# Recurrent attention and a GELU feed-forward on one core: another tiling, another order of transfers, and a list schedule of small groups

## The chip, the cores and the metric

The kernel runs on one core of a Trainium2 chip. The metric is the device time of one execution in microseconds (us). Three runs of the kernel before gave a median of 257.52 us (257.4 to 257.78).

## The reference

For 4 batches of 8 heads, 768 steps of 48 channels, a state of 48 x 48 decays by channel and takes in one outer product at each step; then follow two matrix products with a GELU between them. Cut to what is computed:

```python
f = 1.0 / (1.0 + np.exp(-f_logit))
state = np.zeros((B, H, D, D), dtype=np.float32)
for t in range(S):
    state = f[:, :, t, :, None] * state + np.einsum('bhd,bhe->bhde', k[:, :, t], v[:, :, t])
    y[:, :, t] = np.einsum('bhd,bhde->bhe', q[:, :, t], state)
x = np.ascontiguousarray(y.transpose(0, 2, 1, 3)).reshape(B * S, H * D)
h = x @ w_in                                      # 3072 x 384 by 384 x 2048
g = 0.5 * h * (1.0 + erf(h / np.sqrt(2.0)))
out = g @ w_out                                   # 2048 x 384
```

## The kernel before

The 3072 tokens are 24 chunks of 128 positions, six to a batch. Each chunk needs four loads of 192 KB (f_logit, k, q, v; rows of 48 numbers), an attention part and a feed-forward part.

The decays of a chunk: exponential (L291) and logarithm (L294) on ACT give log f; one matmul with a triangle of -1 (L304) sums it over the positions; two exponentials (L307, L311) give the factors `gt` and `rg`; four matmuls of one column per chunk (L334) and a small exponential (L338) give the decay `gl` over the whole chunk.

The attention, in line order: DVE scales k and q (L314, L318); PE transposes both for four pairs of heads (L361); DVE copies the transposed k into a zero-padded tile in two halves of 48 partitions (L367), ACT copies q (L370); eight score matmuls over all 128 rows (L380), where the zero rows of `kb` blank out the other head of the pair; DVE applies the causal mask (L384). The state is formed by L397, decayed on DVE and GpSimd (L408 to L414) and cast (L421). The output is written with channels on partitions, so that each of eight matmuls (L435) and four state reads (L439) streams 128 positions; four DVE casts (L448, L451), three of them on 32 partitions, make `xT`, the input of the feed-forward.

The feed-forward works on groups of 1, 1, 2, 4, 4, 4, 4 and 4 chunks. "F1" is L473 (weights `win` stationary, `xT` streaming, 384 matmuls in all), GELU is L477 on ACT, "F2" is L488 (`gT` stationary, `wout` streaming 384 columns, 384 matmuls), then a copy on ACT (L492) and a store issued from SP (L494). F1 and F2 of all groups share four PSUM banks with the cumulative sums; the transposes have one bank (`tp`), the output one (`yp`).

The order is made by a planner, `Plan.run`: every operation has an engine, a duration, a priority and its dependences, and the one that can start earliest is placed next; each engine then runs its list in that fixed order. In the second half of `tile_hgrn2_outer__then__act_gelu_exact_kernel` locks are added: the exponentials of group g wait for the last GELU of group g-2 (`gate`), and the F1 and GELU of a group of four wait for the cumulative sums and exponentials of the next group (`lockpe`, `lock`). Loads of chunks are issued from SP, `win` (24 pieces of 16 rows, `load_win`) and `wout` (4 pieces) from GpSimd.

Of the kernel before, what the change touches and what calls it, by code (L numbers as in the profile page):

```python
# [14 lines left out]
class Ring:  # L15


    def __init__(self, bufs, make=None, fixed=None):
        self.bufs, self.make, self.fixed, self.order = bufs, make, fixed, []

    def new(self, **kw):
        return Buf(self, kw)


class Buf:
    def __init__(self, ring, kw):
        self.ring, self.kw, self.users, self.slot, self.handle = ring, kw, [], None, None

    def ready(self):

        r = self.ring
        if self.slot is not None or len(r.order) < r.bufs:
            return 0.0
        old = r.order[len(r.order) - r.bufs]
        t = 0.0
        for u in old.users:
            if u.end is None:
                return None
            t = max(t, u.vis)
        return t  # L40

    def take(self):
        if self.slot is None:
            self.slot = len(self.ring.order) % self.ring.bufs
            self.ring.order.append(self)

    def t(self):
        if self.handle is None:
            r = self.ring
            self.handle = r.fixed[self.slot] if r.fixed else r.make(**self.kw)  # L50
        return self.handle


LAT = {"PE": 0.28, "ACT": 0.12, "DVE": 0.12, "POOL": 0.15, "DMA": 2.0}
SWITCH = 1.28


class Op:
    __slots__ = ("eng", "dur", "fn", "bufs", "prio", "deps", "table", "start", "end", "vis", "seq", "name")


class Plan:

# [4 lines left out]
    def add(self, eng, dur, fn, rd=(), wr=(), bufs=(), prio=0.0, deps=(), table=None, name=""):  # L68
        o = Op()
        o.eng, o.dur, o.fn, o.bufs, o.prio, o.table, o.name = eng, dur, fn, tuple(bufs), prio, table, name  # L70
        o.start = o.end = o.vis = None
# [17 lines left out]
    def run(self):  # L89
        free = {e: 0.0 for e in LAT}  # L90
        act = None
        left = list(self.ops)
        placed = []
        while left:
            best = None
            for o in left:
                t, ok = free[o.eng], True
                for d in o.deps:
                    if d.end is None:
                        ok = False  # L100
# [14 lines left out]
                if o.table and act and o.table != act:  # L115
                    x += 2 * SWITCH
# [13 lines left out]
            for b in o.bufs:  # L130
                b.take()
            left.remove(o)
            placed.append(o)
        placed.sort(key=lambda o: (o.start, o.seq))
        self.placed = placed
        return placed


@with_exitstack
def kernel(  # L140
# [18 lines left out]
    P2 = H // 2  # L159
    KO = 3  # L160
    VB = 144
    PSUM = bass.MemoryType.PSUM
    SIZES = [1, 1, 2, 4, 4, 4, 4, 4]
    NG = len(SIZES)
    first = [sum(SIZES[:i]) for i in range(NG)]

    ctx.enter_context(tc.manual_schedule())
    one = ctx.enter_context(tc.tile_pool(name="one", bufs=1))
    ld = ctx.enter_context(tc.tile_pool(name="ld", bufs=8))
    lg = ctx.enter_context(tc.tile_pool(name="lg", bufs=3))  # L170
    el = ctx.enter_context(tc.tile_pool(name="el", bufs=3))
    at = ctx.enter_context(tc.tile_pool(name="at", bufs=3))
    fx = ctx.enter_context(tc.tile_pool(name="fx", bufs=3))
# [385 lines left out]
```

## Time and profile before

| | before |
|---|---|
| median of three runs | 257.52 us |
| the profiled execution, its span | 260.6 us |
| PE busy | 199.9 us, 77% |
| ACT busy | 152.8 us, 59% |
| DVE busy | 124.3 us, 48% |
| GpSimd busy | 58.9 us, 23% |
| mean granted TensorE clock | 0.895 |
| moved by DMA | 27.00 MB |

The profiled execution has no other time of its own than its span, from the first to the last instruction. It is 3.1 us above the median of the runs, which were not profiled. Busy time of PE counts a matmul from its start to its modelled end, so a busy PE can still be slow; the granted clock, 1.0 for 2.4 GHz and 0.5 for 1.2 GHz, stands beside it. All times in rows are microseconds from the start of the span unless marked ns.

### The profile page before, as it was taken

How to read it: one execution, taken by the hardware profiler on the slowest of the kernel's cores; microseconds unless marked ns; L12 is line 12 of the kernel's file. 1: busy time of each engine (PE TensorE's matmuls, PEld its weight loads, DVE VectorE, ACT ScalarE, POOL GpSimd, SP SyncE). 2: the span in 40 equal slices, each digit the busy share in tenths (PEclk: the TensorE clock that was granted, in tenths of full speed). 3: DMA queues.
4: the chain of work that ended last, by engine and by line, in shares of the span. 5: the costliest groups of instructions: out<-in, count | busy, mean ns of one | idle time of the engine just before them, and what ended most of it. 6: DMA issues, size and time to landing. Idle time of an engine off the chain costs nothing.

```text
span 260.6 us, 4299 instructions
## 1 busy us (share of the span) xinstructions
PE 199.9 (77%) x1611; PEld 130.5 (50%) x1624; DVE 124.3 (48%) x268; ACT 152.8 (59%) x243; POOL 58.9 (23%) x129
## 2 busy tenths in 40 slices
PE   0420739799157769898799999088996999999994
PEld 0310737577036555565475656045664665564462
DVE  5430057730049897993379720038973799200000
ACT  5620575545783852879735851977789456626911
POOL 8863052311020142330133300011130312000000
PEclk9999956999957576999689999759999899999999
DMA  8999919489999999998849302000000010011011
GB/s 140 187 190 184 146 14 168 64 182 202 215 188 186 187 166 193 188 164 132 170 107 209 64 0 93 30 1 0 3 0 33 30 64 0 0 63 60 0 60 60
DMA packets 106195, 27.00 MB, mean 104 GB/s; under 512 B 100672, under 2 KB 105792, under 8 KB 106176
## 3 DMA queue, kind: packets, MB, share of 16 engines
q1 hardware_dynamic: 103296, 23.60, 52.8%
q0 software_dynamic: 2880, 3.15, 8.0%
q8 instruction: 12, 0.20, 0.3%
q14 instruction: 7, 0.06, 0.1%
HBM read 25.17 MB, written 4.72 MB: 115 GB/s over the span
## 4 chain that ended last, share of the span: by engine, by line
PE 55%; ACT 16%; DVE 10%; DMA 8%; issue 5%; POOL 3%; ACTq 0%; POOLq 0%; DVEq 0%
PE hps L473 21%; PE hps L488 19%; DMA win<-in_moe_w_in_dram 7%; PE tp L361 4%; PE yp L435 3%; PE aps L380 3%; ACT lf L294 3%; ACT L294 2%; DVE xT L451 2%; ACT fl L291 2%; DVE kb L367 2%; ACT L291 2%; DMA wout<-in_moe_w_out_dram 2%; ACT qT L370 2%; PE hps L304 2%
## 5 line engine op out<-in xcount | busy, mean ns | idle before, releaser
L473 PE MATMUL hps<-xT,win 128*128 128x512 bf16 (+2 forms) x371 | 73.1, 341 | 13.5 <-DMA win<-in_moe_w_in_dram 11.5
L488 PE MATMUL hps<-wout,gT 128*128 128x384 bf16 x384 | 70.2, 337 | 1.7 <-DMA wout<-in_moe_w_out_dram 1.7
L477 ACT ACTIVATE gT<-hps 128x512 bf16<-128x512 f32 x96 | 55.1, 600 | 26.7 <-PE hps L473 24.4
L473 PEld LDWEIGHTS <-win 128*128 128x128 bf16 x384 | 34.7, 104 | 36.1 <-issue 10.8
L488 PEld LDWEIGHTS <-gT 128*128 128x128 bf16 x384 | 38.0, 101 | 28.1 <-issue 6.3
L314 DVE TENSOR_TENSOR kp<-kt,rg 128x384 bf16<-128x384 f32 x24 | 13.8, 574 | 71.5 <-ACT rg L311 71.2
L492 ACT ACTIVATE osb<-hps 128x384 f32<-128x384 f32 x24 | 11.7, 489 | 42.2 <-PE hps L488 42.2
L384 DVE TENSOR_TENSOR am<-aps,mask 128x512 bf16<-128x512 f32 x48 | 31.3, 687 | 8.2 <-PE aps L380 7.7
L414 POOL TENSOR_TENSOR tn<-rr,gl 128x384 f32<-128x384 f32 x16 | 13.4, 835 | 85.3 <-DVE rr L412 85.3
L370 ACT ACTIVATE qT<-tp 128x512 bf16<-128x512 bf16 x24 | 14.3, 596 | 29.8 <-PE tp L361 19.5
L304 PE MATMUL hps<-lf,trin 128*128 128x384 bf16 x24 | 9.2, 429 | 24.4 <-ACT lf L294 21.6
L380 PE MATMUL aps<-qT,kb 128*128 128x128 bf16 x192 | 19.1, 239 | 9.8 <-DVE kb L367 4.9
L326 POOL CAST vp<-vt 128x384 bf16<-128x384 f32 x24 | 12.3, 514 | 55.6 <-issue 24.5
L367 DVE COPY kb<-tp 48x512 bf16<-48x512 bf16 x48 | 20.2, 421 | 8.0 <-ACT qT L370 5.5
L435 PE MATMUL yp<-am,vp 128*128 128x128 bf16 x192 | 22.4, 239 | 1.3 <-DVE am L384 1.3
L380 PEld LDWEIGHTS <-kb 128*128 128x128 bf16 x192 | 14.3, 108 | 17.2 <-DVE kb L367 13.5
L451 DVE CAST xT<-yp 32x128 bf16<-32x128 f32 x72 | 20.6, 286 | 1.2
L435 PEld LDWEIGHTS <-vp 128*128 128x128 bf16 x192 | 17.3, 107 | 7.1 <-issue 2.3
L421 POOL CAST sb<-tn 48x192 bf16<-48x192 f32 x40 | 15.0, 376 | 13.7 <-DVE tn L408 11.7
L439 PE MATMUL yp<-qT,sb 128*128 128x128 bf16 x80 | 16.9, 236 | 0.0
L448 DVE CAST xT<-yp 96x384 bf16<-96x384 f32 x24 | 13.3, 552 | 6.6 <-PE yp L439 4.7
L334 PEld LDWEIGHTS <-lf 128*128 128x128 bf16 x96 | 3.9, 103 | 22.5 <-issue 22.3
(40 smaller groups left out, 197.1 us busy)
## 6 DMA issues: line engine op xcount, KB each, us to landing
fl<-in_f_logit_dram SPq DMA_DIRECT2D x24, 192.0 KB, 4.5
kt<-in_k_dram SPq DMA_DIRECT2D x24, 192.0 KB, 4.5
qt<-in_q_dram SPq DMA_DIRECT2D x24, 192.0 KB, 4.5
vt<-in_v_dram SPq DMA_DIRECT2D x24, 192.0 KB, 4.5
out_dram<-osb SPq DMA_DIRECT2D x24, 192.0 KB, 1.9
win<-in_moe_w_in_dram POOLq DMA_DIRECT2D x24, 64.0 KB, 5.6
wout<-in_moe_w_out_dram POOLq DMA_DIRECT2D x4, 384.0 KB, 5.5
```

The source lines that it names most:

```text
L304: P.add("PE", 0.17, lambda gps=gps, j=j: nc.tensor.matmul(gps.t()[:, 0:H * D], trin, lf.t()[:, j, :, 0:D], start=True, stop=True), rd=[("l ...
L367: P.add("DVE", 0.42, lambda hh=hh: nc.vector.tensor_copy(kb.t()[64 * hh:64 * hh + D, :, hh, :], tp.t()[64 * hh:64 * hh + D, 0]), rd=[("tk" ...
L370: P.add("ACT", 0.6, lambda: nc.scalar.activation(qT.t(), tp.t()[:, 1], AF.Copy), rd=[("tq", n)], wr=[("qT", n)], bufs=[tp, qT], prio=pr + ...
L380: nc.tensor.matmul(ap_.t()[:, i * C:(i + 1) * C], kb.t()[:, p, hh, :], qT.t()[:, p, :], start=True, stop=True)
L384: P.add("DVE", 0.69, lambda ap_=ap_, am=am: nc.vector.tensor_tensor(am.t(), ap_.t().rearrange("p (h t) -> p h t", t=C), mask.unsqueeze(1). ...
L421: nc.gpsimd.tensor_copy(dst[:, :, :, 16 * hh:16 * hh + 16], tn.t()[64 * hh:64 * hh + D, :, D * hh:D * hh + D] .rearrange("q p (g y) -> q p ...
L435: nc.tensor.matmul(yp.t()[:, p, :], vwin(vp.t(), 2 * p + hh), ams[half].t()[:, 2 * (p % 2) + hh, :], start=(hh == 0), stop=(hh == 1 and c ...
L439: nc.tensor.matmul(yp.t()[:, p, :], osb.t()[:, p, :], qT.t()[:, p, :], start=False, stop=True)
L451: P.add("DVE", 0.29, lambda kk=kk: nc.vector.tensor_copy(xT.t()[96:128, kk, cols()], yp.t()[32 * kk:32 * kk + 32, 3, :]), rd=[("yp", n, 1) ...
L473: nc.tensor.matmul(hps.t()[:, i * tok:(i + 1) * tok], win[:, kk, fo * 128:(fo + 1) * 128], xT.t()[:, kk, 0:tok], start=(kk == 0), stop=(kk ...
L477: acts.append(P.add("ACT", 0.6, lambda u=u, hps=hps: nc.scalar.activation(view()[:, u * pk:(u + 1) * pk, :].rearrange("p a b -> p (a b)"), ...
L488: nc.tensor.matmul(op.t()[:, 0:d_model], view()[:, fo, s_ * C:(s_ + 1) * C], wout[:, fo, :], start=(fo == 0), stop=(fo == FO - 1))
```

## The change

The arithmetic stays; tiling, buffers, transfers and order are new.

- Outputs have positions on partitions: the masked scores are now the stationary operand, and v (48 columns per head) streams. One cast (`yb`) and three transposes on PE (`xmm`), with one copy of 384 elements, make `xT`.
- The transposed k and q leave PSUM in one DVE copy (`kq`). Score matmuls contract over 64 rows: head hh of a pair lies in partitions 64hh to 64hh+63 and writes a PSUM bank of its own.
- `win` comes in four column quarters, F1 waits for its quarter alone, and the hidden units are taken in steps of four columns (`col`); `wout` rows are permuted to match, so that a partition reads four whole rows.
- One list, `LOADS`, orders all input transfers: chunks 0 to 3, `win`, chunk 4, half of `wout`, chunk 5, the rest, then chunks 6 to 23. Where the queue changes between SP and GpSimd, the transfer waits for one two or three places earlier.
- Groups are of 1 and 2 chunks; exponentials and logarithms come per 1 or 2 chunks, in one ACT table that holds both, loaded by name.
- The locks and gates are gone; the planner has other latencies and durations, and picks any free buffer instead of a ring's next. PSUM is split into four banks for F1 and F2, two for scores, and two (`s_m`) for cumulative sums, transposes, state, output and output transpose.

Core of the diff:

```diff
+SIZES = [1, 1, 1, 1, 2, 2, 2, 2, 2, 2, 2, 2, 2, 2]
...
+ELS = [1, 1, 1, 1, 2, 2, 2, 2, 2, 2, 2, 2, 2, 2]
+LOADS = ['c0', 'c1', 'c2', 'c3', 'i0', 'i1', 'i2', 'i3', 'c4', 'o0', 'o1', 'c5', 'o2', 'o3']
+LOADS += [f"c{n}" for n in range(6, 24)]
...
-    SIZES = [1, 1, 2, 4, 4, 4, 4, 4]
...
+    s_fh, s_ap, s_m = Slots(4, banks[0:4]), Slots(2, banks[4:6]), Slots(2, banks[6:8])
...
+    P.add("ACT", 0.0, lambda: nc.scalar.preload_act_table_set("natural_log_exp_and_others"), table="exp", prio=-200)
...
-    r_tp = Ring(1, lambda: pp.tile([C, 2, P2, C], BF16, name="tp"))
-    r_yp = Ring(1, lambda: pp.tile([C, P2, C], F32, name="yp"))
...
-        for hh in range(2):
-            r = (2 * kk + hh) * D + 16 * g if g < 3 else (6 + hh) * D + 16 * kk
-            nc.gpsimd.dma_start(out=win[32 * g + 16 * hh:32 * g + 16 * hh + 16, kk, :],
-                                in_=moe_w_in[r:r + 16, :])
...
+            o.inst = issue()
+            if i and order[i - 1][0] != eng:
+                back = 3 if eng == "pool" else 2
+                for j in range(i - back, -1, -1):
+                    if order[j][0] != eng and order[j][1].inst is not None:
+                        tc.add_manual_dep(
+                            o.inst.ins, order[j][1].inst.ins.name,
+                            mybir.DependencyInfo(mybir.DependencyClass.Sync, mybir.DependencyReason.DATA),
+                            reason="one transfer after another")
+                        break
...
+    win_src = moe_w_in.rearrange("(kk p) f -> p kk f", p=C)
+    wo_src = moe_w_out.rearrange("(r p j) m -> r p j m", r=4, j=4)
...
+    for what in LOADS:
...
+        elif what[0] == "i":
+            load("pool", what, lambda m=m: nc.gpsimd.dma_start(
+                out=win[:, :, 512 * m:512 * m + 512], in_=win_src[:, :, 512 * m:512 * m + 512]),
...
+        else:
+            load("pool", what, lambda m=m: nc.gpsimd.dma_start(out=wout[:, 4 * m:4 * m + 4, :], in_=wo_src[m]),
...
+                def cum(gps=gps, lf=lf, j=j):
+                    nc.tensor.matmul(gps.t()[:, 0:HD], trin, lf.t()[:, j, :, 0:D], start=True, stop=True)
+                    for p in range(P2):
+                        nc.tensor.matmul(gps.t()[:, HD + p:HD + p + 1], lf.t()[:, j, 2 * p:2 * p + 2, :], negcol,
+                                         start=True, stop=True, skip_group_check=True)
...
+                P.add("ACT", 0.40, lambda gps=gps, rg=rg: nc.scalar.activation(
+                    rg.t(), gps.t()[:, 0:HD], AF.Exp, scale=-1.0),
+                    rd=[("g", n)], wr=[("rg", n)], bufs=[gps, rg], table="exp", prio=pr, name=f"RG{n}")
...
+        P.add("DVE", 0.61, lambda: nc.vector.tensor_copy(kq.t(), tpv()),
...
+        def amm():
+            for p in range(P2):
+                for hh in range(2):
+                    r = slice(64 * hh, 64 * hh + 64)
+                    nc.tensor.matmul(aps[hh].t()[:, p * C:(p + 1) * C], kq.t()[r, 0, p, :], kq.t()[r, 1, p, :],
+                                     start=True, stop=True)
...
-            P.add("DVE", 0.42, lambda hh=hh: nc.vector.tensor_copy(
-                kb.t()[64 * hh:64 * hh + D, :, hh, :], tp.t()[64 * hh:64 * hh + D, 0]),
...
-        P.add("ACT", 0.6, lambda: nc.scalar.activation(qT.t(), tp.t()[:, 1], AF.Copy),
...
+        def ymm():
+            on = True
+            if c:
+                for p in range(P2):
+                    nc.tensor.matmul(yp.t()[:, 96 * p:96 * p + 96], kq.t()[:, 1, p, :], osb.t()[:, p, :],
+                                     start=on, stop=False, skip_group_check=True)
+                    on = False
+            for hh in range(2):
+                for p in range(P2):
+                    h = 2 * p + hh
+                    nc.tensor.matmul(yp.t()[:, D * h:D * h + D], ams[hh].t()[:, p, :], vb.t()[:, D * h:D * h + D],
+                                     start=on, stop=(hh == 1 and p == P2 - 1), skip_group_check=True)
+                    on = False
...
+        P.add("DVE", 0.475, lambda: nc.vector.tensor_copy(yb.t(), yp.t()[:, 0:HD]),
...
+        def xmm():
+            for i in range(KO):
+                nc.tensor.transpose(xpv()[:, i, :], yb.t()[:, i * C:(i + 1) * C], ident)
...
+        P.add("DVE", 0.27, lambda: nc.vector.tensor_copy(xT.t()[:, :, j * C:(j + 1) * C], xpv()),
...
-        P.add("DVE", 0.55, lambda: nc.vector.tensor_copy(xT.t()[0:96, :, cols()], yp.t()[0:96, 0:3, :]),
-              rd=[("yp", n, 0), ("yp", n, 1)], wr=[("x", n, 3)], bufs=[yp, xT], prio=pr + 2, name=f"X{n}")
-        for kk in range(KO):
-            P.add("DVE", 0.29, lambda kk=kk: nc.vector.tensor_copy(
-                xT.t()[96:128, kk, cols()], yp.t()[32 * kk:32 * kk + 32, 3, :]),
...
+        def col(fo):
+            return win[:, :, 512 * (fo // 4):512 * (fo // 4) + 512].rearrange("p kk (c j) -> p kk j c", j=4)[:, :, fo % 4, :]
...
+                        nc.tensor.matmul(hps.t()[:, i * tok:(i + 1) * tok], col(fo)[:, kk, :],
+                                         xT.t()[:, kk, :], start=(kk == 0), stop=(kk == KO - 1))
...
-        if g >= 2 and SIZES[g - 2] == 4:
-            G[g]["gate"] = [G[g - 2]["lastgelu"]]
...
-            if SIZES[g - 1] == 4:
-                G[g - 1]["lock"] = G[g]["lastexp"]
-                G[g - 1]["lockpe"] = G[g]["cums"]
...
+    for ph in PHASES:
+        lo, hi = map(int, ph[1:].split(":"))
+        if ph[0] == "X":
+            gate = decays(lo, hi, [])
+            for n in range(lo, hi):
+                attn(n)
...
+            for g in range(lo, hi):
+                got += ffn_group(g, [])
...
+        if o.table and state.get("t") != o.table:
+            state["t"] = o.table
+            if o.dur:
+                nc.scalar.preload_act_table_set({"exp": "natural_log_exp_and_others", "gelu": "gelu_and_others"}[o.table])
```

How this moves instructions is seen at three places. On ACT, before, the start of the decays of a group of four: `fl` is f_logit, `lf` its logarithm, `hps` a PSUM bank, `qT` the copy of the transposed q.

```order
L492 ACTIVATE osb<-hps 128x384 x2
L291 ACT_TABLE_LOAD
L291 ACTIVATE fl<-fl 128x1536
L294 ACT_TABLE_LOAD
L294 ACTIVATE lf_92<-fl 128x32x48
L311 ACT_TABLE_LOAD
L311 ACTIVATE rg<-hps 128x384
L307 ACTIVATE gt<-hps 128x384
L338 ACTIVATE gl<-hps 128x16
L311 ACTIVATE rg<-hps 128x384
L307 ACTIVATE gt<-hps 128x384
```

After, one such phase between the GELUs of two groups (`gT` is the GELU's output, L504 the copy of an output).

```order
L490 ACTIVATE gT_180<-ps_184 128x512
L531 ACT_TABLE_LOAD
L341 ACTIVATE rg_131<-ps_190 128x384
L344 ACTIVATE gt_128<-ps_190 128x384
L347 ACTIVATE gl_133<-ps_190 128x4
L319 ACTIVATE fl_93<-fl_93 128x768
L504 ACTIVATE osb_165<-ps_185 128x384
L323 ACTIVATE lf_99<-fl_93 128x16x48
L341 ACTIVATE rg_129<-ps_189 128x384
L344 ACTIVATE gt_126<-ps_189 128x384
L347 ACTIVATE gl_134<-ps_189 128x4
L504 ACTIVATE osb_166<-ps_186 128x384
```

Three table loads at the start of a group's decays are one now, and the decays of later chunks and the copies of finished outputs stand among each other. The whole list of ACT has 14 table loads.

On GpSimd, before, the weights: `vp` is the cast v, `sb` the cast state.

```order
L254 DMA win<-in_moe_w_in_dram 16x2048 x6
L326 CAST vp_101<-vt 128x8x3x16
L254 DMA win<-in_moe_w_in_dram 16x2048 x6
L421 CAST sb_107<-tn 48x4x3x16 x2
L254 DMA win<-in_moe_w_in_dram 16x2048 x12
L326 CAST vp_102<-vt 128x8x3x16
L326 CAST vp_103<-vt 128x8x3x16
L414 TENSOR_TENSOR tn<-rr,gl 128x384
L421 CAST sb_108<-tn 48x4x3x16
L259 DMA wout<-in_moe_w_out_dram 128x4x384
```

After, the same place.

```order
L423 TENSOR_TENSOR tn_156<-rr_152,gl_134 128x384
L428 CAST sb_159<-tn_156 48x4x48 x2
L305 DMA win<-in_moe_w_in_dram 128x3x512
L358 CAST vb_119<-vt_88 128x384
L305 DMA win<-in_moe_w_in_dram 128x3x512
L423 TENSOR_TENSOR tn_154<-rr_153,gl_135 128x384
L428 CAST sb_157<-tn_154 48x4x48
L305 DMA win<-in_moe_w_in_dram 128x3x512
L428 CAST sb_157<-tn_154 48x4x48
L309 DMA wout<-in_moe_w_out_dram 128x1536
L358 CAST vb_120<-vt_89 128x384
L309 DMA wout<-in_moe_w_out_dram 128x1536 x2
```

The 24 pieces of `win`, 12 of them ahead of the first state cast, became four, behind the casts of the first three chunks; `wout` follows them at once.

On SP, before, the transfers of chunk 4 and the first store: `fl`, `kt`, `qt`, `vt` are loads, `out_dram` the stores of finished outputs.

```order
L277 DMA fl<-in_f_logit_dram 128x8x48
L281 DMA kt<-in_k_dram 128x8x48
L281 DMA qt<-in_q_dram 128x8x48
L281 DMA vt<-in_v_dram 128x8x48
L494 DMA out_dram<-osb 128x384
L277 DMA fl<-in_f_logit_dram 128x8x48
L281 DMA kt<-in_k_dram 128x8x48
```

After, the same, from chunk 4's v on.

```order
L302 DMA vt_89<-in_v_dram 128x8x48
L299 DMA fl_93<-in_f_logit_dram 128x8x48
L302 DMA kt_74<-in_k_dram 128x8x48
L302 DMA qt_82<-in_q_dram 128x8x48
L302 DMA vt_90<-in_v_dram 128x8x48
L299 DMA fl_94<-in_f_logit_dram 128x8x48
L302 DMA kt_75<-in_k_dram 128x8x48
L302 DMA qt_83<-in_q_dram 128x8x48
L506 DMA out_dram<-osb_163 128x384
L506 DMA out_dram<-osb_164 128x384
L302 DMA vt_91<-in_v_dram 128x8x48
L299 DMA fl_94<-in_f_logit_dram 128x8x48
```

The first store stood between chunks 4 and 5; the first two stand now ahead of the v load of chunk 6. On PE, F1 and F2 pieces stand between the attention steps up to chunk 23; behind its last transpose come 20 F2 matmuls and then four times 48 F1 and 32 F2.

## Rows read from the trace of the kernel before

**Rows 1.** The page's busy time, share and instructions of each engine.
```profile
PE 199.9 (77%) x1611; PEld 130.5 (50%) x1624; DVE 124.3 (48%) x268; ACT 152.8 (59%) x243; POOL 58.9 (23%) x129
```

**Rows 2.** Stages: length, busy PE, PEld, DVE, ACT, POOL, then clock, DMA share, GB/s.
```profile
0.00:53.00 53.00, 24.00 (x252) 19.91 (x253) 22.72 (x48) 25.52 (x38) 26.07 (x65) 0.90 0.93 135
53.00:66.50 13.50, 13.35 (x102) 9.60 (x101) 1.45 (x5) 6.42 (x12) 1.40 (x3) 1.00 1.10 204
66.50:98.00 31.50, 17.60 (x172) 13.52 (x172) 20.94 (x45) 22.34 (x33) 6.79 (x14) 0.68 1.27 189
98.00:152.90 54.90, 50.96 (x411) 31.73 (x417) 39.14 (x86) 35.57 (x59) 13.99 (x28) 0.90 0.84 144
...
163.40:180.00 16.60, 9.35 (x79) 5.79 (x80) 6.04 (x12) 13.11 (x19) 2.01 (x4) 0.69 0.03 12
180.00:226.00 46.00, 43.05 (x363) 26.74 (x366) 33.99 (x75) 33.61 (x56) 8.61 (x17) 0.96 0.05 18
226.00:260.60 34.60, 31.16 (x176) 17.03 (x174) 0.00 (x0) 14.11 (x26) 0.00 (x0) 1.00 0.13 46
```

**Rows 3.** The chain of waits, long pieces: start, length, what.
```profile
20.70 5.51 DMA win<-in_moe_w_in_dram
...
46.01 4.88 DMA wout<-in_moe_w_out_dram
...
66.94 1.28 ACT L291
...
69.74 1.28 ACT L294
```

**Rows 4.** The chain again, runs of PE matmuls at full clock.
```profile
52.30 0.67 PE hps L473 x12
52.97 0.65 PE hps L488 x4
...
55.91 5.24 PE hps L473 x48
...
89.85 0.40 PE hps L334 x16
...
187.68 0.45 PE tp L361 x8
...
226.06 10.40 PE hps L488 x64
```

**Rows 5.** ACT by line and shape: count, busy us, mean ns, idle before it.
```profile
L370 ACT ACTIVATE qT<-tp 128x512 bf16<-128x512 bf16 x24 | 14.3, 596 | 29.8 <-PE tp L361 19.5 <-DVE kb L367 9.4 <-PE yp L439 0.9
...
L294 ACT ACT_TABLE_LOAD x8 | 10.3, 1283 | 0.1
...
L338 ACT ACTIVATE gl<-hps 128x4 f32<-128x4 f32 x2 | 0.4, 182 | 0.0
```

**Rows 6.** DVE by line and shape.
```profile
L451 DVE CAST xT<-yp 32x128 bf16<-32x128 f32 x72 | 20.6, 286 | 1.2
L367 DVE COPY kb<-tp 48x512 bf16<-48x512 bf16 x48 | 20.2, 421 | 8.0 <-ACT qT L370 5.5 <-PE tp L361 1.5
...
L448 DVE CAST xT<-yp 96x384 bf16<-96x384 f32 x24 | 13.3, 552 | 6.6 <-PE yp L439 4.7 <-PE yp L435 1.3
```

**Rows 7.** Timeline of ACT at the start: the first load's end.
```profile
3.96 0.52 ACT L291 ACTIVATE fl<-fl 128x384 f32<-128x384 f32 x1 [1.94 <-DMA fl<-in_f_logit_dram]
```

**Rows 8.** Two more stages, columns as in rows 2.
```profile
7.00:26.00 19.00, 4.25 (x30) 2.92 (x30) 5.13 (x11) 5.65 (x9) 11.30 (x25) 1.00 1.28 186
...
98.00:147.00 49.00, 45.11 (x370) 28.43 (x375) 36.27 (x80) 31.14 (x52) 13.49 (x27) 0.89 0.94 162
```

**Rows 9.** The chain's last piece.
```profile
257.30 0.49 ACT osb L492
```

**Rows 10.** PE by line and shape: matmuls and weight loads.
```profile
L473 PEld LDWEIGHTS <-win 128*128 128x128 bf16 x384 | 34.7, 104 | 36.1 <-issue 10.8 <-DMA win<-in_moe_w_in_dram 6.4
...
L380 PE MATMUL aps<-qT,kb 128*128 128x128 bf16 x192 | 19.1, 239 | 9.8 <-DVE kb L367 4.9 <-ACT qT L370 4.8
```

More of the change, by code (lines that the diff above doesn't have):

```diff
@@ L12, with __init__, new, free @@
 ALU = mybir.AluOpType
[L15 to L22, printed above, removed]
[L25 to L55 removed]
+LAT = {"PE": 0.25, "ACT": 0.16, "DVE": 0.14, "POOL": 0.12, "DMA": 1.0}
+TABLE = 1.28
+class Slots:
+    def __init__(self, n, tiles=None):
+        self.n, self.tiles = n, tiles
+        self.who = [None] * n
+    def new(self):
+        return Buf(self)
+    def free(self):
+        out = []
+        for i, b in enumerate(self.who):
+            t = 0.0
+            if b is not None:
+                for u in b.users:
+                    if u.end is None:
+                        t = None
+                        break
+                    t = max(t, u.vis)
+            if t is not None:
+                out.append((t, i))
+        return sorted(out)
+class Buf:
+    __slots__ = ("slots", "users", "slot")
+    def __init__(self, slots):
+        self.slots, self.users, self.slot = slots, [], None
+    def t(self):
+        return self.slots.tiles[self.slot]
 class Op:
[L59 removed]
+    __slots__ = ("eng", "dur", "fn", "bufs", "prio", "deps", "table", "start", "end", "vis", "seq", "name",
+                 "left", "outs", "inst", "gate")
 class Plan:
@@ L263 @@
+    for i in range(3):
+        P.add("DVE", 0.2, lambda i=i: nc.vector.memset(
+            s_sb.tiles[i].rearrange("p a b -> p (a b)").bitcast(F32), 0.0), wr=[f"sbz{i}"], prio=-70)
+    z_lf = [f"lfz{i}" for i in range(3)]
+    z_kp, z_qp = [f"kpz{i}" for i in range(NQ)], [f"qpz{i}" for i in range(NQ)]
+    z_sb = [f"sbz{i}" for i in range(3)]
+    G = [dict(xT=s_xT[SIZES[g]].new(), gT=s_gT[SIZES[g]].new()) for g in range(NG)]
     grp = {}
@@ new lines, with load, fn @@
+    n = 0
+    els = []
+    for s in ELS:
+        els.append(dict(ns=list(range(n, n + s)), fl=s_fl.new(), lf=s_lf.new()))
+        for j in range(s):
+            X[n + j].update(el=els[-1], j=j)
+        n += s
+    for n in range(NCH):
+        for nm in ("kt", "qt", "vt"):
+            X[n][nm] = s_in[nm].new()
+    order = []
+    def load(eng, what, issue, wr, bufs, dur, name):
+        i = len(order)
+        o = P.add("DMA", dur, None, wr=wr, bufs=bufs, prio=i, name=name)
+        o.table = None
+        order.append((eng, o))
+        def fn():
+            o.inst = issue()
[7 more added lines that the diff above has]
+                            reason="one transfer after another")
+                        break
+        o.fn = fn
+        return o
```

434 lines of the change are left out of this document (181 added, 253 removed).

## The prediction

> **What bounds the kernel now.** I read the page's busy line first, then the table of stages, then the chain of waits for what starts and ends each stage, then the groups by line for prices. PE is the busiest engine, yet busy for only 199.9 of 260.6 us [rows 1]. Cut into stages [rows 2], its 60.7 us of idle time lie mostly in three places: 29.0 us before 53 us, 13.9 us from 66.5 to 98 us, and 7.3 us from 163.4 to 180 us. In the last two the granted clock was 0.68 and 0.69 besides, so what PE did there cost half as much again. At 226 to 257 us nothing interrupts PE at all.
>
> The chain says what ends each gap [rows 3]. Until 26.3 us F1 (the first matmul of the second half) waits for the 24 pieces of w_in; at 46 us F2 (the second) waits for the last piece of w_out, issued only then. At 66.9 us begins the other kind of gap: table load, exponential, table load, logarithm, while the planner's locks hold F1 of the finished group of four back until the cumulative sums of the next four are done.
>
> **How the sum is made.** It is in the span of the one profiled execution, 260.6 us, in which all durations were taken; the three runs have a median of 257.52 us, so a run is 0.988 of the profiled span, and I multiply at the end.
>
> Paces of PE at full clock [rows 4]: 4 passes per 384 columns of F2 in 0.65 us, so 0.1625 us each (64 in 10.40 us agree); 48 F1 matmuls of 256 columns in 5.24 us, 0.109 us each; 12 of 128 columns in 0.67 us, 0.056 us each; eight 128-column transposes in 0.45 us; 16 weight loads, each with a one-column matmul, in 0.40 us, so 0.025 us is the floor of a small one.
>
> F1 after the change is 192 x 0.056 + 480 x 0.109 = 63.1 us; F2 is 384 x 0.1625 = 62.4 us: as before, since columns are neither added nor removed.
>
> Attention on PE, per chunk: eight transposes 0.45; eight 64-row score tiles, which no row shows, between 0.23 (each pair side by side) and 0.45 (one after another), I take the middle, 0.34; four state matmuls and four state reads of 96 columns, each at most 0.22, I take 0.17 for either (absent in a sixth of the chunks); eight output matmuls that now stream 48 columns instead of 128, between 8 x 0.025 = 0.20 and 8 x 0.056 = 0.45, I take 0.33; three new transposes 0.17; cumulative sum 0.16 + 4 x 0.025 = 0.26. Together 1.9 us (1.65 to 2.2).
>
> **ACT, DVE and the other parts.** ACT has 27 table loads of 1.283 us [rows 5]; the row shows eight, and three groups like it have eight, six and five. The new order has 14, as exponential and logarithm share a table: -16.7 us. The qT copies go: -14.3 us [rows 5]. Logarithms, exponentials and the small decay vectors come in more pieces: 28 more at some 0.18 us [rows 5] add 5. ACT falls from 152.8 to about 127 us. DVE loses 20.6 us of 32-partition casts and 20.2 of half copies [rows 6]. It gains 24 copies of 1024 bf16 elements, priced between one half copy (0.42) and two (0.84), I take 0.7; and 24 of 384 elements, between 0.29 and 0.55 [rows 6], I take 0.4: about 124 - 41 + 26 = 109 us. Neither engine is then near PE's 171 us. That they run beside PE hides them; if the cover fails, it is in the mixed stage below. GpSimd's casts and state multiplies stay; its zero fills go to DVE, at the start, beside the first loads.
>
> **Stage A, loads until about 47 us.** The first load's exponential began at 3.96 us, and loads alone ran at 204 GB/s (0.96 us per 192 KB) [rows 7, 2]. Sixteen loads (chunks 0 to 3) end at 3.96 + 15 x 0.96 = 18.4 us. Eight weight pieces of 384 KB, at 186 GB/s as early on [rows 8], cost 2.1 us each, 17 in all; chunks 4 and 5 cost 7.7. That makes 43 us. At each of four changes of queue the next transfer now waits for one some places earlier, 0 to 2 us each; I take 1: 47 us. PE needs only F1 and F2 of four chunks (21 us) and six attentions (11 us) there, and F1 begins with the first quarter, near 21 us. What waits: GpSimd's first w_in transfer waits for chunk 3's k load, and behind it stand that chunk's state multiply and casts; SP's first stores stand ahead of chunk 6's v load. Both lie beside transfers here.
>
> **Stage B, attention and the second half mixed.** By PE's order the last attention ends with F1 480 and F2 236 instructions done, of which 192 and 64 belong to A: 288 x 0.109 + 172 x 0.1625 + 18 x 1.9 = 31.4 + 28.0 + 34.2 = 93.6 us at full speed. The stretches of before in which the same kinds of work mix gave PE 50.96 of 54.9 us at clock 0.90 and 43.05 of 46.0 at 0.96 [rows 2], 0.84 and 0.90 as a product. I take 0.89, near the second, since ACT and DVE are lighter and the locks are gone: 105.2 us, to 152 us. The loads allow it: 72 at 0.96 to 1.05 us (204 and 189 GB/s in rows 2) and some 14 stores end at 125 to 137 us, and a chunk's chain of some 10 us follows. Banks too: cumulative sums, transposes, state, output and output transpose now share two banks, held about 6.2 us per chunk, 3.1 us on each, against 5.8 us per chunk.
>
> **Stage C, the second half alone.** Left are 192 x 0.109 + 148 x 0.1625 = 45.0 us, and no attention. Then the last copy, 0.49 us from 257.30 [rows 9], and 2.8 us to the end of the span, as now. Sum: 47 + 105.2 + 45.0 + 3.3 = 200.5 us of span, times 0.988 = 198 us.
>
> **Two rules against the trace.** A matmul by itself takes 239 ns where a stream takes 56 [rows 10], so an array that empties loses about 0.18 us. The Trainium skill (TensorEngine Tiling, Key Properties) says that a change of tiling mode drains the array, which this trace cannot show as it has no small tiles. By that rule every score step costs two drains; it is a rival below.
> A weight load reads 128 adjacent columns in every row of before, and lasts 104 ns [rows 10] but hides. The new w_in is read in steps of four elements. The Trainium skill (TensorE: Matmul & The Clock Gate, Weight-path perf modes) keeps the fast load for steps up to 1,024 elements; by it the sum stays, and no row here bears on it. It is why I hold the strided rival for unlikely.
>
> **The rivals.**
> *Denser.* The order follows real durations and B runs at 0.97 of full speed: 96.5 us, span 191.8, time 189.5. For it: 226 to 257 us is gapless. Against: no mixed stretch of before came over 0.90.
> *Loads bound.* If a load costs 1.21 us, as at the 162 GB/s of 98 to 147 us [rows 8], 72 loads and stores end at about 148 us, the last attention at 158: span 206.5, time 204. Against: the loads of that stretch also waited for buffers.
> *Drains.* 36 changes of mode in B at 0.18 us: 6.6 us, time 204.5. For it: the 64-row tiles stand between full-array work each time. Against: the sum takes the middle price of the scores already, 0.11 us over the least.
> *Strided weights.* If a strided load cannot hide behind 256 columns, each F1 matmul costs 0.109 + 0.104: 480 times 0.10 is 48 us more, time 246; with a mixed stage at 0.84 it nears the old time. Against: a load of 104 ns hides in a stream of 56 ns per matmul now [rows 4, 10].
> *Slower: two banks stall the fixed order.* PE's order is fixed, so a transpose that waits for one of the two shared banks holds F1 behind it; PE idles, and the clock falls, as from 66.5 to 98 us, where busy share times clock was 0.56 x 0.68 = 0.38. At that rate B takes 246 us, time 338. It decides once B's product falls under 93.6 / 165 = 0.57, where the span is again 260.6. For it: that stretch of before had one transpose bank. Against: banks are held for half the time.
> That the change does not do what it says (table loads kept) is excluded by the order, which has 14.
>
> **Chances.** Forecast 0.48 (its own range 192 to 203 us), denser 0.20, loads 0.12, drains 0.10, strided 0.05, stalled order 0.05. The range takes in denser, loads and drains with their bounds: low, A at 43, B without loss, 184.9 x 0.988 = 183; high, A at 51, B at 0.84 (112 us) and the drains, 218 x 0.988 = 215. I give 185 to 216 us. About 0.2% (0.5 us) is what a measurement can tell from no change. Faster 0.95, within it 0.01, slower 0.04: strided counts as faster in nearly all its cases, stalled as slower in most.
>
> **What would show it.** Right: F1 begins near 21 us, PE busy and clock over 0.9 from 47 us on without a gap of several us, 14 table loads, DVE near 109 and ACT near 127 us, the last attention near 152 us, then 45 us of PE alone. Wrong: PE waiting for the output copies or the shared banks in B, F1 at more than 0.11 us per 256 columns, eight scores in more than 0.45 us, or loads that end after 145 us.

## The result and the profile after

The changed kernel takes 229.0 us (median of four runs, 227.11 to 229.28) against 257.65 us (four runs of the kernel before beside it): ratio 0.885, 95% interval [0.881, 0.890]. It is faster by about 29 us, and 31 us slower than the forecast, outside its range. The profiled run has a span of 227.1 us and a time of its own of 228.91 us. Times of the experiments below are medians of fast runs alone: five runs in a slower state, two of them far outside (994.25 and 684.56 us), are left out, by which the run without hand-overs stands at 210.4 us where later expectations have 212.16.

The page's busy time, which answers to [rows 1]:

```profile
PE 187.8 (83%) x1984; PEld 147.7 (65%) x1984; DVE 103.8 (46%) x210; ACT 126.5 (56%) x234; POOL 49.0 (22%) x99
```

The stages of after, columns as in [rows 2] (stretch, length, busy PE, PEld, DVE, ACT, POOL, clock, DMA share, GB/s). The third row ends where the first F1 matmul of 256 columns begins, the fourth where the last attention is done:

```profile
21.00:33.00 12.00, 5.94 (x60) 4.59 (x58) 4.52 (x8) 2.29 (x3) 5.02 (x8) 1.00 0.41 57
33.00:52.00 19.00, 10.95 (x121) 10.69 (x122) 0.92 (x2) 4.57 (x8) 2.91 (x6) 1.00 0.92 160
52.00:72.25 20.25, 18.15 (x205) 12.82 (x203) 7.94 (x15) 10.49 (x20) 3.44 (x7) 1.00 0.65 129
72.25:178.35 106.10, 97.29 (x1157) 77.02 (x1158) 75.27 (x140) 75.75 (x141) 30.90 (x59) 0.97 0.77 145
178.35:223.40 45.05, 45.01 (x340) 35.26 (x338) 0.36 (x1) 23.52 (x41) 0.00 (x0) 1.00 0.11 40
```

Read from the bottom: stage C is 45.0 us, as forecast; stage B 106.1 us, forecast 105.2. Nearly all of the miss in the span lies above them: stage A ends at 72.25 us instead of 47, and from 21 to 33 us PE was busy half the time while the DMA engines moved 57 GB/s. They were not full there; they had been given nothing to move. The clock of 1.00 in the first two rows is not what the matmuls show: the trace has no clock record before 50.4 us, and until then F1's matmuls of 128 columns start 0.107 us apart, twice the 0.056 us of [rows 4], which is the pace of the lower level (1.2 GHz); PE had been waiting again and again.

The chain of waits, for paces (answers to [rows 4] and [rows 9]):

```profile
173.56 0.17 PE ps L442 x4
173.73 0.20 PE ps L448 x8
173.93 0.33 PE ps L392 x8
...
178.18 0.17 PE ps L462 x3
178.35 3.25 PE ps L500 x20
181.60 5.24 PE ps L485 x48
186.84 5.20 PE ps L500 x32
...
223.45 0.49 ACT osb L504
```

L485 is F1, L500 F2: 48 F1 matmuls in 5.24 us, to the digit what they took with adjacent weights. Eight 64-row scores (L392) take 0.33 us, eight outputs (L448) 0.20, state reads (L442) 0.17.

Groups by line and shape (busy us, mean ns | idle before), which answer to [rows 5, 6, 10]:

```profile
L485 PEld LDWEIGHTS <-win 128*128 128x128 bf16 x672 | 67.0, 119 | 16.5 <-DMA win<-in_moe_w_in_dram 14.1 <-DVE xT L464 0.6
...
L531 ACT ACT_TABLE_LOAD x13 | 16.7, 1283 | 0.2
L383 DVE COPY kq<-ps 128x1024 bf16<-128x1024 bf16 x24 | 16.3, 685 | 4.9 <-PE ps L378 3.4 <-ACT lf L323 0.9 <-issue 0.6
...
L464 DVE COPY xT<-ps 128x384 bf16<-128x384 bf16 x24 | 8.5, 352 | 6.7 <-PE ps L462 6.5
...
L228 ACT ACT_TABLE_LOAD x1 | 1.3, 1283 | 0.7 <-PEq L549 0.7
```

Now to the place of the miss. The timeline of GpSimd (start, length, idle before and what ended it): L305 issues the quarters of w_in, L309 those of w_out.

```profile
18.03 0.93 POOL L305 DMA_DIRECT2D win<-in_moe_w_in_dram  x1
22.87 0.81 POOL L305 DMA_DIRECT2D win<-in_moe_w_in_dram  x1
...
30.64 0.78 POOL L305 DMA_DIRECT2D win<-in_moe_w_in_dram  x1 [6.41 <-PE ps L485]
38.96 0.80 POOL L305 DMA_DIRECT2D win<-in_moe_w_in_dram  x1 [6.28 <-PE ps L485]
...
51.77 0.53 POOL L309 DMA_DIRECT2D wout<-in_moe_w_out_dram  x1 [9.29 <-DMA kt<-in_k_dram]
```

The third and fourth quarter wait for F1, which is reading an earlier quarter. PE's timeline is the other half of the circle: it waits for a quarter that had to wait for it.

```profile
27.70 2.75 PE L485 MATMUL ps<-xT,win 128*128 128x128 bf16 x24 [2.76 <-DMA win<-in_moe_w_in_dram]
35.38 1.36 PE L485 MATMUL ps<-xT,win 128*128 128x128 bf16 x11 [4.93 <-DMA win<-in_moe_w_in_dram]
...
44.76 10.83 PE L485 MATMUL ps<-xT,win 128*128 128x128 bf16 x143 [5.67 <-DMA win<-in_moe_w_in_dram]
```

And the waits of SyncE's queue (sum, times, longest), which stands for the weights at the hand-overs and then for the outputs that it is to store:

```profile
SPq L506 <- ACT osb L504: 79.5, 20, 12.6
SPq L299 <- DMA win<-in_moe_w_in_dram: 19.4, 1, 19.4
SPq L299 <- DMA wout<-in_moe_w_out_dram: 14.5, 2, 8.3
```

### The profile page after: what moved, and what is told of

It is laid out like the page before. It is cut to its first block, busy times and chain, and to the rows that moved or that the text cites. A ratio compares the mean times of both kernels' runs of the same rounds, so it can differ in the third digit from the quotient of the medians.

```text
span 227.1 us, 4959 instructions
## 1 busy us (share of the span) xinstructions
PE 187.8 (83%) x1984; PEld 147.7 (65%) x1984; DVE 103.8 (46%) x210; ACT 126.5 (56%) x234; POOL 49.0 (22%) x99
## 5 line engine op out<-in xcount | busy, mean ns | idle before, releaser
L485 PE MATMUL ps<-xT,win 128*128 128x256 bf16 (+1 forms) x672 | 77.4, 275 | 13.8 <-DMA win<-in_moe_w_in_dram 13.4
L485 PEld LDWEIGHTS <-win 128*128 128x128 bf16 x672 | 67.0, 119 | 16.5 <-DMA win<-in_moe_w_in_dram 14.1
L490 ACT ACTIVATE gT<-ps 128x512 bf16<-128x512 f32 x96 | 55.1, 600 | 37.0 <-PE ps L485 34.0
L500 PE MATMUL ps<-wout,gT 128*128 128x384 bf16 x384 | 68.9, 326 | 0.0
L500 PEld LDWEIGHTS <-gT 128*128 128x128 bf16 x384 | 35.7, 98 | 20.1
L396 DVE TENSOR_TENSOR am<-ps,mask 128x512 bf16<-128x512 f32 x48 | 31.3, 684 | 3.5 <-PE ps L392 3.2
L504 ACT ACTIVATE osb<-ps 128x384 f32<-128x384 f32 x24 | 11.8, 490 | 31.9 <-PE ps L500 31.9
L358 POOL CAST vb<-vt 128x384 bf16<-128x384 f32 x24 | 13.1, 546 | 58.6 <-DMA vt<-in_v_dram 58.5
L454 DVE CAST yb<-ps 128x384 bf16<-128x384 f32 x24 | 13.3, 555 | 22.3 <-PE ps L448 22.1
L383 DVE COPY kq<-ps 128x1024 bf16<-128x1024 bf16 x24 | 16.3, 685 | 4.9 <-PE ps L378 3.4
L341 ACT ACTIVATE rg<-ps 128x384 f32<-128x384 f32 x24 | 11.9, 496 | 10.7 <-PE ps L337 10.5
L531 ACT ACT_TABLE_LOAD x13 | 16.7, 1283 | 0.2
L354 DVE TENSOR_TENSOR qp<-qt,gt 128x384 bf16<-128x384 f32 x24 | 15.4, 640 | 0.0
L392 PE MATMUL ps<-kq 64*128 64x128 bf16 x192 | 10.4, 233 | 2.5 <-DVE kq L383 2.5
```

What stands on the lines that cost most here:

```text
L354: P.add("DVE", 0.475, lambda x=x, gt=gt: nc.vector.tensor_tensor(x["qp"].t()[:, :, 0:D], x["qt"].t(), gt.t().rearrange("p (h d) -> p h d", ...
L358: P.add("POOL", 0.47, lambda x=x: nc.gpsimd.tensor_copy(x["vb"].t(), x["vt"].t().rearrange("p h d -> p (h d)")), rd=[("vt", n)], wr=[("vb" ...
L383: P.add("DVE", 0.61, lambda: nc.vector.tensor_copy(kq.t(), tpv()), rd=[("tk", n), ("tq", n)], wr=[("kq", n)], bufs=[tp, kq], prio=pr + 4, ...
L396: P.add("DVE", 0.61, lambda hh=hh: nc.vector.tensor_tensor(ams[hh].t(), aps[hh].t().rearrange("p (h t) -> p h t", t=C), mask.unsqueeze(1). ...
L454: P.add("DVE", 0.475, lambda: nc.vector.tensor_copy(yb.t(), yp.t()[:, 0:HD]), rd=[("yp", n)], wr=[("yb", n)], bufs=[yp, yb], prio=pr + 2, ...
L485: nc.tensor.matmul(hps.t()[:, i * tok:(i + 1) * tok], col(fo)[:, kk, :], xT.t()[:, kk, :], start=(kk == 0), stop=(kk == KO - 1))
```

## The experiments

Theory after the result: stage A is long because transfers that could run are held back, by three things: `win` is one tile, so that a write into one quarter waits for reads of another; the hand-overs between SyncE and GpSimd; and stores that wait for F2 at the head of SyncE's list with loads behind them. Rivals: the DMA engines or PE's own work bound stage A, and the held transfers cost nothing. "A" and "B" below are the ends of the two stages (after: 72.25 and 178.35 us). Ratios are to the kernel before on the same chip.

**One tile for each quarter of w_in.**

```diff
-    win = one.tile([C, KO, d_ff], BF16, name="win")
+    wins = [one.tile([C, KO, 512], BF16, name=f"win{i}") for i in range(4)]
```

> w_in in four tiles of 512 columns instead of one tile of 2048; the order of every engine's list stays. In the changed kernel the first w_in quarter is issued at 18.0 us and the last is used by F1 from 44.8 us, because the third and fourth transfer wait for F1 on an earlier quarter (12.7 us of GpSimd waiting for L485). Theory, waits through the shared tile: with tiles of their own the four follow each other at 2.1 us and the last lands near 18 + 8.4 + 5 = 31 us, 13 us earlier; the time falls by 13 to 20 us, to 209 to 216. Rival one, the transfers are slow by themselves (5 us landing each, hand-overs between queues): within 3 us of 229. Rival two, the gain is given back at the stores that stand ahead of loads in SP's list, and at the rate of the loads: 219 to 224.

Measured 217.27 us, ratio 0.842 [0.835, 0.849], 11.7 us less than after; A 63.02, B 166.99. GpSimd's and PE's timelines:

```profile
24.12 0.78 POOL L305 DMA_DIRECT2D win<-in_moe_w_in_dram  x1
27.45 0.80 POOL L305 DMA_DIRECT2D win<-in_moe_w_in_dram  x1
36.68 0.58 POOL L309 DMA_DIRECT2D wout<-in_moe_w_out_dram  x1 [8.04 <-DMA kt<-in_k_dram]
```

```profile
31.30 7.67 PE L485 MATMUL ps<-xT,win 128*128 128x128 bf16 x132 [0.91 <-DMA win<-in_moe_w_in_dram]
```

The last quarter is issued at 27.45 instead of 38.96 us, and F1 of the first four chunks is done at 39.0 instead of 55.6. Nothing was changed but which tile a transfer writes and F1 reads: the wait was the tile's. Stage A gained 9.2 us, less than F1's 16: w_out was now held at the hand-over (8.04 us), and F2 stood for it. Part of F1's gain is pace: it ran at 0.107 us a matmul until 50.4 us in the changed kernel, here until 28 us.

**Stores from ScalarE.**

```diff
-  lambda n=n, osb=osb: nc.sync.dma_start(out=out[n * C:(n + 1) * C, :], in_=osb.t())
+  lambda n=n, osb=osb: nc.scalar.dma_start(out=out[n * C:(n + 1) * C, :], in_=osb.t())
```

> Stores of the output are issued from ACT instead of SP; all else as in the changed kernel. There the v load of chunk 6 stands behind two stores that wait for the copies of the first outputs, and was issued at 67.8 us, 8 us after the load before it. Theory, loads held by stores: the loads after it start up to 8 us earlier and the mixed stage, in which GpSimd waits 58 us for v and ACT 16 us for f_logit, ends 3 to 8 us earlier: 221 to 226. Rival, F1 and F2 of the first chunks set that stage and loads only follow: within 1.5 us of 229. Rival two, 24 issues of some 0.35 us on ACT cost as much as they save: 229 to 233.

> Both edits: four tiles for w_in, stores issued from ACT. Theory, the waits through the shared tile are the larger loss and the stores hold the loads behind it: 201 to 210, less than with the tiles alone. If the rate of the loads (192 KB per 1.0 to 1.05 us) sets the end of the mixed stage in both, it comes out within 2 us of the tiles alone. If stores matter only while the tiles hold F1 back, likewise.

By itself 223.4 us, ratio 0.868 [0.857, 0.880] (A 70.84, B 173.24); with the four tiles 214.9 us, 0.830 [0.821, 0.839] (A 62.48, B 164.77). So 5.6 us alone and 2.4 us on top of the tiles, most of it in stage B: with a waiting store out of the way, loads of later chunks come sooner (chunk 6's v is issued at 63.1 us instead of 67.8).

**No hand-overs (with the four tiles).**

```diff
-            if i and order[i - 1][0] != eng:
+            if False:
```

> Four tiles for w_in, and no waits between the transfers of SP and GpSimd: weights and chunk loads run beside each other. Theory, hand-overs cost 1 to 2 us each as forecast (four to six of them): 4 to 8 us less than the tiles alone. Rival, ordered transfers are worth more than the hand-overs: weights issued early share the engines with chunks 1 to 3, attention of the first chunks comes later, and the time is 0 to 6 us above the tiles alone.

Measured 210.4 us, ratio 0.815 [0.806, 0.824], 6.9 us less than with the tiles alone; A 56.96, B 160.91. The timeline of SyncE's queue now shows the next hold:

```profile
40.62 1.16 SPq L302 DMA_DIRECT2D qt<-in_q_dram  x1
51.47 1.01 SPq L506 DMA_DIRECT2D out_dram<-osb  x2
52.53 0.46 SPq L302 DMA_DIRECT2D vt<-in_v_dram  x1
```

From 41.8 to 51.5 us the queue stands for the first store. Chunk 6's v load behind it was ready.

**Both, and then all weights issued at once.**

> The tiles of e4 and no hand-overs, and stores issued from ACT. In e4 SP issues q of chunk 6 at 40.6 us and then waits until 51.5 us for the first output copy, as stores stand ahead of the v load of chunk 6. Theory, SP's order still holds stage A and the first loads of stage B: the first F1 of 256 columns comes 2 to 4 us earlier than its 57.0 us, the time falls from 212.2 to 206 to 210. Rival, the last w_out piece (F2's last quarter) ends stage A whatever SP does: within 1.5 us of 212.

The second's further edit:

```diff
+    early = [o for o in P.placed if o.name in LOADS and o.name[0] in "io"]
...
+        if o is early[0]:
+            for w in early[1:]:
+                o.fn()
+                o = w
```

> As e5, but GpSimd issues all eight weight transfers one behind the other where the first one stood; in e4 the last w_out piece stood behind a cast that waited 11.3 us for the v load of chunk 5 and was issued at 42.5 us, the piece before it at 30.2. Theory, GpSimd's in-order list delays the last piece: F2 of the first four chunks can end 4 to 8 us earlier and the time falls by 2 to 6 us against e5. Rival, the transfer rate is the limit: the weights only push chunks 4 and 5 back (4 x 2.1 us), and eight issues hold the state cast of chunk 2 back some 5 us; the time is 0 to 4 us above e5.

The first (stores from ScalarE without hand-overs) took 216.01 us, ratio 0.836 [0.829, 0.844]; the second, in which GpSimd also issues all eight weight transfers together, 221.73 us, 0.858 [0.847, 0.868]. Both are slower than with the stores on SyncE (210.4 us), against what was expected. ScalarE's and PE's timelines of the second show why:

```profile
50.72 0.49 ACT L504 ACTIVATE osb<-ps 128x384 f32<-128x384 f32 x1 [0.16 <-PE ps L500]
63.21 1.39 ACTq L506 DMA_DIRECT2D out_dram<-osb  x2
64.65 0.49 ACT L504 ACTIVATE osb<-ps 128x384 f32<-128x384 f32 x1 [13.44 <-DMA kt<-in_k_dram]
```

```profile
56.07 0.84 PE L485 MATMUL ps<-xT,win 128*128 128x256 bf16 x6 [0.45 <-DVE xT L464]
72.47 0.48 PE L335 MATMUL ps<-lf,trin 128*128 128x384 bf16 x1 [15.55 <-ACT lf L323]
73.32 2.73 PE L485 MATMUL ps<-xT,win 128*128 128x256 bf16 x12
```

The output was ready at 51.2 us, but its store was issued at 63.2, and what let ScalarE go on were *loads* (the row names one of k). In the trace each transfer issued from SyncE or ScalarE carries one of eight semaphores, in turn, and goes out when the transfer that carried it before has landed: the first store has that of the f_logit load issued at 58.84 us, which landed near 62.9. With loads running ahead, a store inherits their lateness; on SyncE that delays other transfers, on ScalarE it held the next logarithm (four stores with three such waits between 51.2 and 71.6 us), and through it PE for 15.55 us, in the first of the two versions for 8.15 us. After that PE runs at half pace (12 F1 matmuls in 2.73 us against 1.31).

**Stores on SyncE, further back in its list.**

```diff
+    late = [o for o in P.placed if o.name in ("st0", "st1", "st2", "st3")]
+    placed = [o for o in P.placed if o not in late]
+    i = [o.name for o in placed].index("ldvt8") + 1
+    placed[i:i] = late
```

> Beside the four w_in tiles without hand-overs (212.16 us), the first four stores stand behind chunk 8's loads in SyncE's list, still on SyncE. Theory: there SyncE stood from 41.8 to 51.5 us for the first store while the next loads were ready and the DMA share fell to 0.30; loads then come some 9 us earlier, stage A ends at 50 to 54 us instead of 57, stage B keeps its 104 us, time 206 to 210 us. Rival: loads that run ahead crowd the last w_out piece, issued at 42.5 us, as when the stores were moved to ScalarE (216.01 us): stage A ends at 57 us or later and the time is 212 us or more.

And the last piece of w_out ahead of the cast of chunk 5's v:

```diff
+    vc = placed.pop(names.index("VC5"))
+    placed.insert([o.name for o in placed].index("o3") + 1, vc)
```

> As the run before it, and GpSimd issues the last w_out piece ahead of the cast of chunk 5's v, for which it stood 11.3 us. Theory: the piece is issued near 31 us instead of 42.5, F2 of the first chunks ends some 5 us earlier, stage A ends at 47 to 51 us, the time is 202 to 206 us. Rival: the transfers share 16 engines that are full from 20 to 45 us, so the piece only trades places with chunk 5's loads: no gain over the run before, within 1 us.

And all stores, without the edit before:

```diff
+        while j < len(placed) and loads < 9 and placed[j].name not in (f"O{n + 4}", f"st{n + 1}"):
+            loads += placed[j].name[:2] == "ld"
+            j += 1
+        if loads:
+            placed.insert(j, o)
+            del placed[i]
```

> Four w_in tiles without hand-overs, and now every store, not only the first four, stands up to nine loads further back in SyncE's list (never behind the copy that reuses its buffer). With the first four alone the time was 208.6 us, and the DMA engines still fell to 0.7 and 0.1 of their time near 62 to 70 us, while SyncE stood for the store of chunk 4. Theory (a store that stands ahead of ready loads costs what its wait keeps idle): that hole closes, stage B shortens by 1 to 5 us, 203 to 208 us. Rival (PE is no longer waiting for loads in stage B, so the hole costs nothing): 208 to 209 us; the stores that come later may make chunk 4's to 11's copies wait for their buffers, up to 212 us.

The first four stores behind chunk 8's loads: 208.6 us, ratio 0.808 [0.805, 0.811]. The time came as the theory had it, but not the place: A is 57.19 us, unchanged, and B 158.10; the gain (1.8 us by the runs, 2.8 us at B's end) lies in stage B. The last piece of w_out ahead of the cast: 208.2 us, 0.806 [0.804, 0.809], no gain, as the rival had it. All stores up to nine loads back: 205.81 us, 0.796 [0.790, 0.801], A 57.03, B 155.11. This is the fastest version, 23 us under the changed kernel. Its stage A, by windows (F1's first instruction to its last wait for w_in, then to A's end):

```profile
24.60:35.50 10.90, 8.78 (x127) 8.34 (x125) 2.48 (x5) 5.38 (x9) 4.62 (x9) 1.00 1.20 199
35.50:57.00 21.50, 19.42 (x224) 14.09 (x224) 7.94 (x15) 12.12 (x22) 3.66 (x7) 1.00 1.19 201
```

PE is busy for 28.2 of 32.4 us. Until 28.2 us it ran at half pace here too, as the first of two F1 lines shows (0.107 us a matmul, then 0.060), although the row says 1.00:

```profile
24.61 3.85 PE L485 MATMUL ps<-xT,win 128*128 128x128 bf16 x36
...
31.23 2.87 PE L485 MATMUL ps<-xT,win 128*128 128x128 bf16 x48 [0.74 <-DMA win<-in_moe_w_in_dram]
```

What is left of stage A is mostly PE's own work. The DMA engines, at 200 GB/s, are as full there as in the fullest stages of [rows 2], so no run here shows whether A could end sooner if PE were faster.

**Thirteen more table loads (with the four tiles, without hand-overs).**

```diff
+                nc.scalar.preload_act_table_set("sigmoid_and_others")
                 nc.scalar.preload_act_table_set({"exp": ...
```

> Four w_in tiles without hand-overs (212.16 us), with every one of the 13 later table loads preceded by a load of an unrelated table: 27 loads as in the kernel before, 13 x 1.283 = 16.7 us more on ScalarE, nothing else changed. Theory (the loads lay beside PE in the new order): 0 to 5 us slower, 212 to 217 us. Rival (exponential and logarithm head the chain of each chunk and the fixed order of PE waits for them): the most of 16.7 us, 222 to 229 us.

Measured 218.57 us, ratio 0.845 [0.840, 0.850], 8.2 us more for 16.7 us of ScalarE. Stage B of the profiled run by windows:

```profile
56.30:166.66 110.36, 97.50 (x1158) 76.68 (x1159) 74.81 (x140) 89.17 (x152) 29.88 (x59) 0.98 0.77 140
```

110.4 us against 103.95 without them, all that this profiled run lost. ScalarE is busy for 89 of 110 us, so it is not the bound, and yet 0.4 us (by the profiled runs) to 0.5 us (by the medians) of each microsecond reaches PE. Both theories missed: the loads lay neither wholly beside PE nor wholly on its path.

**Two parts in the kernel before.** One table for exponential and logarithm (named as in the change, 12 loads instead of 27); and, apart from it, the kernel before without its gate and locks.

```diff
+        if o.table and state.get("t") != o.table:
+            state["t"] = o.table
+            nc.scalar.preload_act_table_set({"exp": "natural_log_exp_and_others", "gelu": "gelu_and_others"}[o.table])
```

> The kernel before with one part of the change alone: the table that holds exponential and logarithm is loaded by name, so 12 table loads stand in ACT's list instead of 27. Theory, two of three loads of each phase lie on the chain before the cumulative sums of the next group (five phases of groups of four): five times 2.6 us and part of the three small phases, 10 to 16 us less: 242 to 248. Rival, ACT is busy for 59% only and the loads lie beside PE work: within 3 us of 258.

```diff
-            G[g]["gate"] = [G[g - 2]["lastgelu"]]
+            pass
...
-            if SIZES[g - 1] == 4:
+            if False:
```

> The kernel before without its gates and locks (F1, GELU and exponentials wait for their data alone; the planner orders anew, 25 table loads). Theory, the locks make the two gaps of 13.9 and 7.3 us of idle PE at a halved clock: 12 to 25 us less, 233 to 246. Rival, the gaps come from the exponentials themselves and from table loads, and F1 has nothing ready there: 250 to 260.

The shared table alone: 248.7 us, ratio 0.962 [0.954, 0.971]; in the gap of [rows 2] PE got a fifth more work done:

```profile
66.50:98.00 31.50, 21.06 (x208) 15.46 (x208) 24.57 (x52) 16.28 (x29) 7.84 (x16) 0.73 1.25 193
```

Without the locks, in an order that the planner made anew: 273.6 us, ratio 1.059 [1.043, 1.074], slower, and the gap stays (windows):

```profile
66.00:100.00 34.00, 20.05 (x178) 14.39 (x178) 23.21 (x50) 22.54 (x33) 7.85 (x16) 0.67 1.19 190
```

So, with groups of four, the locks alone did not make that gap, and leaving them out by itself gains nothing. The shared table gives 9 to 10 us in the old order; the rest of the gain is shared by the smaller groups, the lighter copies and the new transfers, which were not tried apart.

## Why the prediction was wrong, step by step

**The step that failed is stage A**, "47 us", the sum of transfers. The span was missed by 26.6 us, of which A has 25.25, B 0.9, the tail 0.4. The profiled runs divide A's 25.25, in the order in which the holds were taken away:

- 9.2 us: the tile that all quarters share, with the half pace of PE that came of the waits. The prediction had "F1 waits for its quarter alone" and "F1 begins with the first quarter, near 21 us"; it listed what GpSimd's first w_in transfer waits for, and not what the third and fourth wait for, which was PE.
- 6.1 us: the hand-overs. "0 to 2 us each; I take 1" was the wrong kind of price. A transfer that must wait for another pays that one's whole way to landing (medians of 4.3 to 6.5 us on the page), and what stood behind it in its queue paid too: GpSimd 9.29 us at one of them.
- 10.0 us: what stays when both are gone. It is the sum's own mistake: it ended A with the last transfer, although the 21 us of F1 and F2 that it put from 21 us on end at 42 us by themselves, and part of the 11 us of attention falls between them. Measured (in the fastest version, where A is as long), F1 began at 24.6, PE worked 28.2 us, its first 3.5 at half pace, and waited 4.2: 57.0.

"SP's first stores stand ahead of chunk 6's v load ... Both lie beside transfers" failed as well: moving all stores back gave 4.6 us (210.4 to 205.81) and shortened stage B of the profiled runs from 103.95 to 98.1 us, in which PE's busy share times clock went from 0.91 to 0.96.

**The factor 0.988** cost 4.3 us. The profiled run of after has a time 1.8 us above its span (228.91 and 227.1), as have the versions made from it (205.69 and 203.9), and a run of before with a span of 260.6 us took 262.48. The profiled execution of before was a longer one than the median, not a sign that a run is shorter than its span; the sum should have had 1.8 us added, not 1.2% taken off.

**Stage B, right in size, in part by luck:** product of PE's busy share and clock 97.29 / 106.1 x 0.97 = 0.89, the value taken from [rows 2], though part of what B lost was loads behind waiting stores, which the prediction had put at nothing. The rival with stalls on the two shared banks did not come: the longest waits of PE in B are of 1.9 and 2.1 us, and the cumulative sum stood 2.3 us in all behind ScalarE's read of a bank. **Denser**, at 0.97, is nearly reached where loads no longer wait (94.15 us of PE in 98.1 at clock 1.00 in the fastest version, 0.96). **Loads bound** has a true core, since loads did hold B, but by waits in queues, not by their rate.

**Stage C and the tail, right:** 45.0 and 3.7 us against 45.0 and 3.3.

**Engines, right:** 14 table loads, ACT 126.5 (forecast 127), DVE 103.8 (109); the 1024-element copy 685 ns (0.7), the 384-element one 352 (0.4). Attention on PE came to 1.73 us a chunk for 1.9, and to 1.82 with the loss ahead of the scores that follows. But "that they run beside PE hides them" is true only in part, as the extra table loads show.

**Drains: there, at half the price, and no part of the miss.** The chain's rows cannot show them, since the modelled end of a matmul lies behind the start of the next; the starts do. After, with scores of 64 rows (L392) behind outputs (L448), and the same outputs with F2 behind them:

```profile
173.57 0.36 PE L448 MATMUL ps<-vb,am 128*128 128x48 bf16 x8
173.86 0.40 PE L392 MATMUL ps<-kq 64*128 64x128 bf16 x8
174.19 1.50 PE L485 MATMUL ps<-xT,win 128*128 128x256 bf16 x12
...
176.52 0.36 PE L448 MATMUL ps<-vb,am 128*128 128x48 bf16 x8
176.72 1.46 PE L500 MATMUL ps<-wout,gT 128*128 128x384 bf16 x8
```

Before, four scores of 128 rows (L380), next to F1:

```profile
189.88 0.39 PE L380 MATMUL aps<-qT,kb 128*128 128x128 bf16 x4
190.11 1.46 PE L473 MATMUL hps<-xT,win 128*128 128x512 bf16 x6
```

Eight outputs need 0.20 us ahead of F2 and 0.29 us ahead of scores. Where the 64-row scores did not wait for data (19 of 24 times), they began 0.09 us late, and what followed them at full clock began 0.148 us behind the last start instead of 0.056, 0.09 us late again; before, F1 began 0.056 us behind the last of four scores. Between the two losses the pairs ran side by side, starts 3 to 4 ns apart and the next pair 0.053 us later. So the score's 0.33 us, forecast as 0.34, the middle of two prices, fits by luck: it is the lower price, 0.23, and one loss. The Trainium skill's rule (TensorEngine Tiling, Key Properties) that a change of tiling mode drains the array agrees with the trace, at 0.09 us for each change. Whether it is that, or a weight load (0.09 us too) that cannot hide there, the trace does not tell. The 0.18 us of the prediction came from [rows 10], where 239 ns is the mean length of matmuls that come in fours and eights, not of one by itself. The 36 changes in B come to 3.3 us, half of the rival's 6.6, and one half of that was in the price of the scores.

**Strided weights, right:** F1's pace is unchanged at 5.24 us for 48. The Trainium skill (TensorE: Matmul & The Clock Gate, Weight-path perf modes) keeps the fast load for such steps; the trace agrees, with a mean load of 119 ns where it was 104, still hidden.

## What to carry to other kernels

Bound a stage by its longest chain, the arrival of the last input and then all the work that needs it, before summing its transfers. When data come in pieces so that work can start early, look in the waits of the program whether a write into one piece waits for a reader of another, and give each piece a tile of its own. In a queue that works in order, nothing that waits for compute belongs ahead of transfers that are ready; and moving it to a compute engine's queue can move the wait there (with the stores on ScalarE, 5.6 and 2.4 us were gained while hand-overs held the loads, and 5.6 us lost without them). Check the clock of a stage against the pace of its matmuls, and small losses on PE by starts, not by modelled ends.

## What had not been expected

- Weights that are issued together each take longer to come: the median from issue to landing of a 384 KB piece of w_in and w_out is 5.0 and 6.5 us with hand-overs, 6.8 and 9.3 without, 9.7 and 15.7 when all eight are issued at once.
- After 15.55 us without work the clock stood at 0.5 (1.2 GHz), and stage B of that version took 116.5 us against 108.5 with stores from ScalarE alone.
- Thirteen table loads of 1.283 us cost 8.2 us (6.4 us in stage B of the profiled runs) on an engine that was busy for 60% of its time, 73% in that stage.
- Each change to 64-row tiles, and each change back, cost 0.09 us on PE, which no row of busy time shows.
